# A new table of order, engines and buffers for a two-layer interleaved attention kernel on one core

## The chip, the cores and the metric

The kernel runs on one core of one Trainium2 chip. A core has five engines with queues of their own: PE (TensorE, matrix products into PSUM), DVE (VectorE), ACT (ScalarE), POOL (GpSimd) and SP (SyncE, which here issues nearly all DMAs). The profile shows PE's weight loads as PEld. Each engine works through its queue in order, and waits at an instruction until the semaphores named there have reached a value. The metric is the time of one execution on the device, in microseconds (us); less is better. The median of three runs of the kernel before is 483.39 us.

## The reference

The input x has 2048 tokens of 512 values (bf16), and there are 32 heads of 16 values. Four blocks follow each other, A B A B, each as `x = x + block(layernorm(x))`; both A blocks share their weights, and so do both B blocks.

```
A: q, k, v = x@wq, x@wk, x@wv; four segments of 512 tokens, in order:
     p     = softmax(q k^T * scale + causal mask)      within the segment
     a_mem = phi(q) M / (phi(q) z + 1e-6)              phi(t) = t + 1 if t > 0 else exp(t)
     o     = sigmoid(beta) * a_mem + (1 - sigmoid(beta)) * (p v)
     M, z  = M + phi(k)^T v, z + sum phi(k)            for the next segment
   result o @ wo
B: q, k, v = x@wqkv; pq, pk = q w_phi, k w_phi         per head
     phi_q = [softmax(pq), softmax(-pq)], phi_k likewise
     kv    = sum over ALL tokens of phi_k^T v; z = sum of phi_k
     o     = phi_q kv / (phi_q z + 1e-6)
   result o @ wo
```

The sum over all tokens in B means that no query of B can be finished before the keys of all 2048 tokens are done. This cuts the program in three: up to the first such point, from there to the second, and the end.

## The kernel before, in words

Tokens lie in 16 tiles of 128, four tiles to a segment. The activations X stay in SBUF for the whole run. The program is first recorded as a list of 2864 operations with their reads and writes (`Graph.op`), and each operation knows on which engines it can run. An operation is one instruction on DVE, ACT or POOL, a small group of matmuls on PE, or a DMA. Then `Graph.place` reads a packed table, `ORDER`, with three things for the whole program:

```
order = [self.ops[i] for i in np.frombuffer(raw, "<u2", n)]     # the order of all operations
o.seq, o.eng = k, ENGS[raw[2 * n + o.id]]                        # the engine of each
slots = dict(zip(tiles, raw[3 * n:]))                            # the buffer of each tile
```

`Graph.emit` (line 190) cuts this one order into five queues and sets a wait wherever an operation needs a result of another queue, or a buffer which the tile before it in the same buffer (its `base`) still uses. So the table alone settles what stands behind what on each engine, and which wait ends when.

The steps that matter here, with their places:

- Layer norm, `ln` (line 574): DVE takes statistics of a tile of X (line 577) and combines them (line 578), POOL (or ACT for the first four tiles) takes the root, DVE normalises (lines 594 and 598). The result is transposed by a DMA of SP (`tr`, line 364) or, for some tiles, by PE with an evacuation from PSUM (`tpe`, lines 378, 359 and 360).
- Block A, `a_proj` (line 658): keys and queries of four groups of heads are one pair of operations each (`pair`, lines 330 to 347, eight matmuls in each half, shown at line 341). `evac` (line 358) copies them out of PSUM on ACT (line 359) or DVE (line 360). For each group DVE multiplies the keys by four masks (line 679), which the score products need. V uses the weight WA_v, which POOL or DVE multiplies by a gate first (line 530).
- Block A, `a_att` (line 768): scores on PE (`mm`, line 326), exponentials on ACT (line 351) from PSUM, products with V on PE, the division on DVE (line 847), transposes, output projection and residual (`out_proj`, line 877; the residual is an addition on DVE at line 898 or, where PE has added X itself, a copy).
- Block B: `b_keys` (line 922) and `b_query` (line 987), with exponentials on ACT, sums and products on DVE, and an output projection at the end. The results leave by a DMA of SP for one or two tiles (line 368).

PSUM is four tiles, D0 to D3, of 1024 float32 in each partition, and almost every product goes through one of them. At the start PE multiplies ones for a while (`warm`, line 639: 26 wide operations and some narrower ones) before the first transposes.

The loads of the start are DMAs of SP and ACT at line 457: four single tiles of X, then X in pieces of four tiles (512 KB), then weights, in the table's order.

Of the kernel before, what the change touches and what calls it, by code (L numbers as in the profile page):

```python
# [16 lines left out]
D = 512  # L17
H = 32
# [279 lines left out]
class Kernel:  # L298
# [834 lines left out]
>$jbUTia2NrT*bFujX0lN*opoj1SWniA&0<SfR4M{RVLn^RIzty&#=61^)(r|lVOYslvEHmF3}egLY&L<-W5ZcAn#20AFOZPNvAOIzd&#0OAKS&&u+=OQ+spQ_P!^W
;0tUGtH)MnC0FVQ6!Yej{4TaYX!GTn4BuhkJ0dN8P$`tru7<7lVY#n>U*0Ub)jeTUvAP?k+d{6-LLP3}a$zc+#fwfQ^N<uLx0sWyb3;+%v7=c0!?;r(~f`zO!B&YZA
mQ7~wSw9#LDPc5hfC(@LQo%+T0%Kt+OoMSSp2cRVAq9PB8`wMci6QoeJ}?;8!6LRE5>pad%m_73VI04~2bjnN8vG6xKf)%M0+V4LPGth7vCU8x2Ej%)AIm{S*u(-LH
aWPN4TR}nU<Q0<)uB8jWpQW=+sPzUg6L2KDnM<RgE62E%*Cou4QfIys0;OA9#nz(&;aT~We8vqSs>fZ%78>4W@DcqCM1G*kQib?LudqzVH+%iee4k14$EN)B!T_xFp
CedVLM9-OJNr5fFPI+J7Ez7!yH%)bD;?=fTpkl_CNyo0Y6v>M27GX1;Rm8hycwXEktFXAsk~E5dt9;62eS4#?rtSwgDHyMqCM7;0RlVTVXZsg<04ZBEeDC9Kt{g2nz
# [91 lines left out]
```

## Time and profile before

| what | value |
|---|---|
| runs | 482.28, 483.39 and 484.38 us; median 483.39 |
| profiled execution, first to last instruction | span 481.9 us; no time of its own is listed beside it |
| PE busy | 452.9 us, 94% |
| DVE busy | 438.3 us, 91% |
| ACT busy | 425.9 us, 88% |
| POOL busy | 63.8 us, 13% |
| weight loads of PE (PEld) | 298.4 us, 62% |
| first projection on PE | 13.31 us |
| first score product on PE | 21.16 us |

How to read the profile: busy time counts an engine's own work, not its waits. The end of a matmul is modelled, and matmuls overlap, so PE's busy share says little of how near to its peak PE is; two starts that follow each other say more. A row "x<-y" gives the tile written and the tile read, then count, busy time, mean length in ns, and the idle time just before with what ended it. PEclk is the share of full clock that PE was granted. The chain follows the last instruction back, at each step to what released it.

### The profile page before, as it was taken

Reading aid. Unit: us, or ns where it says so; the run is one execution under the profiler, and the core shown is the slowest. Engines: PE = TensorE matmul, PEld = TensorE weight load, DVE = VectorE, ACT = ScalarE, POOL = GpSimd, SP = SyncE. Lnnn points to the kernel's source line nnn. Section 1 sums busy time; section 2 is a strip of 40 time slices with the busy share of each in tenths; the row PEclk is TensorE's granted clock in tenths of the full one; section 3 lists DMA queues with packets and bytes.
Section 4 is the critical chain, followed back from the end, with each engine's and each line's share of the span. In section 5 each row is a group of like instructions: output and inputs, shape, how many; then the busy total and the mean of one; then the engine's idle time right before and its main releaser. Section 6 shows DMA issues by size and latency. Waiting matters only on the chain.

```text
span 481.9 us, 25218 instructions
## 1 busy us (share of the span) xinstructions
PE 452.9 (94%) x11582; PEld 298.4 (62%) x11582; DVE 438.3 (91%) x920; ACT 425.9 (88%) x560; POOL 63.8 (13%) x145
## 2 busy tenths in 40 slices
PE   8798889999989999998999999999999999999895
PEld 3346665757767677666555677576667666666553
DVE  4998999899889999898999999999999897998883
ACT  2598999999989998578999999999999999776892
POOL 2801120101010110200231041020002020110000
PEclk9999999999999999998999999999999999999799
DMA  8735254350144212200225344432204403100256
GB/s 216 199 83 139 39 90 69 47 86 21 41 68 69 37 15 48 41 1 5 46 52 96 57 72 59 79 67 47 31 4 62 77 16 59 37 12 3 46 93 196
DMA packets 89451, 30.37 MB, mean 63 GB/s; under 512 B 76000, under 2 KB 89344, under 8 KB 89344
## 3 DMA queue, kind: packets, MB, share of 16 engines
q1 hardware_dynamic: 88992, 28.46, 32.1%
q8 instruction: 91, 1.49, 1.3%
q10 hardware_dynamic: 288, 0.26, 0.2%
q0 software_dynamic: 64, 0.02, 0.1%
q14 instruction: 16, 0.13, 0.1%
HBM read 6.32 MB, written 2.10 MB: 17 GB/s over the span
## 4 chain that ended last, share of the span: by engine, by line
PE 54%; DVE 20%; ACT 17%; DMA 3%; issue 2%; SPq 2%; POOL 1%; DVEq 0%
PE D L341 35%; PE D L326 18%; ACT p L351 9%; ACT pF L351 5%; DVE p L635 3%; DVE pQ L679 2%; DVE stats L577 2%; ACT pE L351 2%; SPq L364 2%; DVE p L360 1%; DMA X<-in_A_x_dram 1%; DVE p L598 1%; DVE pK L360 1%; DVE p L847 1%; DMA pX<-p 1%
## 5 line engine op out<-in xcount | busy, mean ns | idle before, releaser
L351 ACT ACTIVATE p<-D 128x1024 bf16<-128x1024 f32 (+1 forms) x276 | 251.5, 956 | 27.5 <-PE D L341 15.9
L351 ACT ACTIVATE pF<-D 128x896 bf16<-128x896 f32 x128 | 117.3, 938 | 2.7 <-PE D L326 2.0
L326 PE MATMUL D<-pK,pQ 64*128 64x256 bf16 (+3 forms) x1536 | 113.9, 243 | 6.1 <-DVE pQ L679 2.3
L326 PEld LDWEIGHTS D<-pK,pQ 64*128 64x128 bf16 x1536 | 54.9, 94 | 45.6 <-ACT p L351 5.8
L326 PE MATMUL D<-pV,pF 64*128 64x34 bf16 x1024 | 75.8, 176 | 1.7 <-ACT pE L351 0.5
L326 PE MATMUL D<-pW,pF 64*128 64x34 bf16 x1024 | 73.0, 176 | 0.5 <-issue 0.5
L585 POOL TENSOR_SCALAR rstd<-mv 128x1 f32<-128x1 f32 x60 | 18.6, 321 | 357.4 <-DVE mv L578 357.4
L341 PE MATMUL D<-pX,WA_k 64*128 64x512 bf16 x256 | 64.7, 376 | 0.7 <-DVE pX L360 0.7
L341 PE MATMUL D<-pX,WA_q 64*128 64x512 bf16 x256 | 64.7, 377 | 0.1
L326 PEld LDWEIGHTS D<-pV,pF 64*128 64x128 bf16 x1024 | 56.8, 93 | 5.3 <-issue 2.2
L326 PEld LDWEIGHTS D<-pW,pF 64*128 64x128 bf16 x1024 | 52.4, 93 | 1.3 <-issue 0.5
L351 ACT ACTIVATE pE<-D 128x768 bf16<-128x768 f32 x64 | 52.5, 830 | 0.8 <-PE D L326 0.4
L326 PE MATMUL D<-pV,p 64*128 64x34 bf16 x1024 | 52.2, 175 | 0.9 <-issue 0.6
L326 PE MATMUL D<-pW,p 64*128 64x34 bf16 x1024 | 51.1, 176 | 0.0
L326 PEld LDWEIGHTS D<-pV,p 64*128 64x128 bf16 x1024 | 46.7, 93 | 2.7 <-ACT p L351 0.5
L326 PE MATMUL D<-tri,two 64*128 64x128 bf16 (+1 forms) x384 | 46.2, 234 | 0.0
L326 PEld LDWEIGHTS D<-pW,p 64*128 64x128 bf16 x1024 | 45.1, 93 | 1.6
L577 DVE BATCH_NORM_STATS2 stats<-X 128x6 f32<-128x512 bf16 x64 | 42.7, 680 | 3.7 <-DMA X<-in_A_x_dram 3.4
L326 PE MATMUL D<-pV,pE 64*128 64x34 bf16 x512 | 45.0, 175 | 0.0
L679 DVE TENSOR_SCALAR pQ<-p,m 128x512 bf16<-128x512 bf16 x128 | 44.2, 366 | 0.1
L326 PE MATMUL D<-pW,pE 64*128 64x34 bf16 x512 | 42.7, 175 | 0.3 <-issue 0.3
L945 DVE TENSOR_REDUCE pS<-p 128x64 f32<-128x1024 bf16 (+1 forms) x36 | 38.6, 1084 | 1.3 <-ACT p L351 1.3
(118 smaller groups left out, 1001.5 us busy)
## 6 DMA issues: line engine op xcount, KB each, us to landing
pW<-pV SPq DMA_DIRECT2D x16, 136.0 KB, 2.8
out_dram<-X SPq DMA_DIRECT2D x7, 256.0 KB, 3.3
X<-in_A_x_dram SPq DMA_DIRECT2D x3, 512.0 KB, 6.4
pX<-in_B_wqkv_dram SPq DMA_DIRECT2D x3, 512.0 KB, 5.2
p<-p SPq DMA_TRANSPOSE x76, 2.6
pX<-p SPq DMA_TRANSPOSE x54, 3.3
WA_k<-in_A_wk_dram SPq DMA_DIRECT2D x2, 256.0 KB, 6.4
WA_q<-in_A_wq_dram SPq DMA_DIRECT2D x2, 256.0 KB, 8.0
```

The lines of the kernel that those rows point to most:

```text
L326: ins = e.matmul(out_ap, lhsT, rhs, start=st, stop=sp, tile_position=(basep(lhsT), basep(out_ap)))
L341: ins = e.matmul(out_ap, lhsT[64 * hf:64 * hf + 64], rhs[64 * hf:64 * hf + 64], start=k == 0 and i == 0, stop=k == 1 and i == len(lists[hf ...
L351: return self.g.op({"act": (dur, lambda e: e.activation(out_ap(), in_ap(), func, scale=scale))}, reads, writes, opens, label=label)
L360: "dve": ((340 if fast else n / 0.96 + 65), lambda e: e.tensor_copy(out_ap(), in_ap()))}
L364: return self.g.op({"sp": (1200.0, lambda e: [e.dma_start(out_ap(), in_ap(), transpose=True)])}, reads, writes, opens, kind="d", lat=1450. ...
L577: v(lambda e: e.bn_stats(self.stats[:, t, :], self.X[:, t, :]), 602, [R("X", t)], [R("st", t)], label="bn")
L585: v(lambda e: e.tensor_scalar(rs, self.mv[:, t, 1:2], LN_EPS, None, op0=ALU.add), 170, [R("mv", t)], [R("rstd", t)], eng="pool", label="rstd")
L598: v(lambda e: e.tensor_scalar(xn.t[:], self.X[:, t, :], self.mv[:, t, 0:1], self.rstd[:, t:t + 1], op0=ALU.subtract, op1=ALU.mult), 300, [ ...
L635: v(lambda e: e.scalar_tensor_tensor(dst.t[:], e_.t[:], 1.0, dst.t[:], op0=ALU.min, op1=ALU.add), 335, [dst, e_], [dst], label="phadd", po ...
L679: fn = lambda e, KM=KM, KT=KT, sl=sl: e.tensor_scalar(KM.t[:, :, sl % 2, :, 64 * (sl // 2):64 * (sl // 2) + 64], KT.t[:].rearrange("p (j h ...
L847: v(lambda e, pvv=pvv, rden=rden, part=part: e.tensor_tensor(part(o).rearrange("p (a h d) -> p a h d", a=2, h=16), pvv()[:, :, :, 0:16], r ...
L945: fn = lambda e, sgn=sgn, eo=eo, Z=Z, n=n: e.tensor_reduce(Z.t[:, 0:64 * n].rearrange("p (k s h) -> p k s h", k=n, s=2)[:, :, sgn, :], eo( ...
```

## The change

The string `ORDER` is replaced; not one line of the program beside it differs. The operations are the same 2864, with the same reads and writes. Decoded, the tables differ so:

- Order: an operation of PE stands 3.3 places from where it stood on its queue on average (at most 29), of ACT 6.1, of DVE 8.5, of SP 5.1, of POOL 4.2.
- Engines: 30 operations change their engine. Copies out of PSUM of 512 columns: 12 from DVE to ACT and 8 from ACT to DVE, transposes with them included; two copies of V (1024 columns) from DVE to ACT; three residual copies of the last 20 us from ACT to DVE; a copy and a fold of weights from DVE to ACT; one gate and two fills with a constant from POOL to DVE.
- Buffers: tiles get other buffers of their pool; the pools and their sizes stay.
- Start: SP issues its two single tiles of X, then four tiles of X, then keys' and queries' weights, WA_v, and the other weights later. DVE takes the statistics of all four single tiles before those of the tiles 4 to 7. The first group's two halves of the key and query projection follow each other on PE, where the second group's first half stood between them. Four of the 26 wide warm-up matmuls stand behind the first transposes.

The diff, cut to its ends (a line is 136 characters of a packed string):

```
--- before.py
+++ after.py
@@ -1127,67 +1127,67 @@
 ORDER = """
-c-rlH1GFW}vTa60y4Ggfwr$(CZQHhO+qP}nw(ag$wYu*)=lb4<KmHrz)!wTzvnn%k=8PGUReP@_tTL;@;<M;1F{{d|vFfY_tI2Ay+N=(%%j&WEtO0At8nMQ#32Vxlv
...
+c-rlH1C%XGw(VN6!dbNo$F^<Twr$(CZQHhO+qP|=^E3B3ef!?q-M_nk|2M{aW4x@Y+>wzHOLMLj5qne;s0>x0DpZ5&Py=d0EvOB3pf1#d`p^IxLL+DlO&~GEhXlYN5fl
...
 """
```

More of the change, by code (lines that the diff above doesn't have):

```diff
@@ L1134 @@
[L1134 to L1137, printed above, removed]
@@ new lines @@
+XFb$-JrBD>dK`_jM`LF~Y!%!TC%b+WE!xfMVGXt{akQ-ORDtHNiUoZ#0!<?8B=7M5haRGEjM23tx*abD~iM{X@C>#N=Au9x6Hp~DcVJ)nK>^K?Tz(-gOYak!y$CCIJ*2
+5n71_iJn&Vv%z7yDr{9F1epzywH+b6_@X!n{}<!$L89kDD<NeK;N`V1LYmyI?2yz_1UH0yU1scaRbXU@6>yd!aOz!Ev||C*m5Mgx?_*a$Jj3(XynF3MRr}bXa$s0zGgD
+N?eEQF%*Je3iifNFbz{<S|sd)lkppV$MH}W%i%&;1jIP2h?Ouo{ea!D7-B<ptbx%nHqFC9I3M4`TbReT!ax*k4ih+^N%k4$vKUw!r{fHq3e%ttmd6TM7wch7tcJBP5mv
+>R7ze9hAZ&yrm>A>X60DCOFe+_=%}^P`Lj!Dxjc^+-#Y1oyw&NmPjInSP+Xp{zKSZO1G=mvTL91C12Cyx#0~_N^whV(Y1S4Zq+yFaqIi{pgoP%?57B<1SI2(_^QD}<Iu
@@ new lines @@
+sH&Yg5hxihQYSj4j1AIT*ub4J-8RwunlY@TZsqYAk4%>v<kmKd~AWya5bjEwQLJ+#oDY6E6P6NCrpaf*=LMS5wHe}K?!g-)?~F<d)$Q`up@TDeHa#JvDs`thJ#|PIIF}
+evns41Ys8|m*cc95VpG<PRb{QPHMYS+>@bVQs<8wtI*Y~PuxTuiC1lswbvB*FAs;)y4zeH?k%ePnSqs*jMZ`#~0lR?Ppe}37Vz7(Ygk8b|co6Hej;s@F#kNB|mWU;0E!
+iP#&DyY3bOjUB0=AGH#wBbiI|&If5{6-g*dn%=Sv-PA@faS*W$Xw$$_lencpA@OUly0GWXD($R)VcyC$JyOgeS2#JI?yBcq}t!!K_%4oyFy>C+o#xvvYVJ(_wn-%m%V9
+Y!J(U?O6xbpM__aaRA%GBEnX-jfJw9tOtwC+Olq}JL}2@v$zzG;?oeeiS1(B*=BYJZ?GM3lO>^~G?d-Ndw7qvV>{S=mYJodm^6&-WV=}ii^5K@EbJ;iz~Ss9%gU~>`?!
@@ new lines @@
+aVV8JXG%g6Sz>zJR#qBHC&JIik1DR!ETWDoH%Uc)==E=xc+aW$=>6Oe>mVwc%%yoE_wGWMA5r1LBd?V@w+2|mKqY%ir}8Q4?2#WG?xwvTeMN9;E1L>Jiw)|ryC>})qZ$
+3656AF>B5C0kA_=m~p`PgzFxjIE?M_!e`p+-xnaqIFb&)ue1tkaeJrREt_sYwAK>sWv5}v^0uEU@fR6J*8)qjxw=^l!~>dMwErJQhMr1nWzV~qh{2cp0f$;1+J%;n1Z#
+XR~QxcvF?<Sy3uIXhI&zN+Dsd04BJ8z*(A1~4$x#)htjb4EE{d4O;nfa(NQ`^+bBCdrX6&V_Olo42_2?Ol$NDqFWC`#PI=fX_K|I;#x#X(rKxNHy`WPxkPgxzx&SBXB7
+9<b*;Tqmuh~*sMuTWDJ*3ZUEE~thv*YxJJ)#qIn$FM&8cF47483Jds2@dvrZkrNQ+cXDRjC}iOyyYxmVv6#II2!pXgKwuVbqt#(-&5QM$u^c&MMJMdPP6jS5}b?p|doR
@@ new lines @@
+hSCI@M1|=b0lj1I*<_kRQ;E@ex<EzfEoG)s^p0{+Q7TPk=r-M<>vV&Na#AkJPo>y#Xv0ghGVDFwqgMPI`#^0u(p}0+1t<>{Bu<5>HNQ!>Xd1QS?fG<iO>gKvePF418ZP
+Jo<)(a;mDi_Fl#S1z`Sg*>vO#<>@5lS|&-8^PEugZLnP=xYxT2Z#l^ReMK8qI8B3ev+cwcVGP+Fdj&nAa7&7pH}9+L255I{+JMn0E(RGc#Ll2nX3@Q(Z&eW#Q>75_n}A
+SWNdgD4lTNWhUVq0^9?59E1xC!T?)=Xv=Eo{v|idDNL#p^-e0cjL)<GM<8W=fn7L?&Cqc3lF8Pd=(GjVW=nX!4(grU>d`h@e&k5n)l+XIpbsb5WbxE=0kZ=UW|t$;+zX
+Ec|jhQ3i15B1#ihG@yUENAH@sv@HCE(=M#8Y9)TiK5nhg;f%5z;l;9P3ac;Qf4lm8i@RGa~k3{QuWSYm<^8$Q6ugI(LP(F=M=TWFKuf(hJIXoPn%d7DXygHx3H}dd2n1
@@ new lines @@
+|&7JPeP(XYq+V5}(Oe@ESZKpUorlEqo<k$QSUMd<l=jqw;7xI$z4S@+o{Ouf=QgI=m5|EY|R~JSJbvBSS2{i8tm=_-0<0*W>m1BEF4J5!?9=K2^lvvH4EEiwB7Ye45zJ
+8}hh3ScHhCycv(f_wXY;9^cFN@%{WLKgJz#oS)za_(2{j;`0Rj5KqXP^K<+pPsC60)BHS7%+K(%`~ttoFY(L#Di08W;tGGuuW_F^%y04Q{3gG_Z}U5Ry12*h^LP9`|Hx
+;Eqw+3)#J}>H;vs*`pYRX-GylfF^9TGH|G|&RSt6A@E>Fm({5k)`U-1|Gi@VKw$zSu-GL3x0r9hEZDxn1vB!oyO(@QJDi?G57F2aa#B7=+|W{Zd-lE^6Mi8&&km@DRs1
+tPMDBBF|DVxd?hvdG0^iHIpO%lIM^L>DncERj`alG$Veu~eiM2}NuXM`V|2L?V$x=9IZ)Zn;dv6=}tCu~lpn+r<u%Oe7a6#6h`B>=t{(UJ(Hji?w2%ST7FAl;W^VC(?^
@@ new lines @@
+lVuQ#dlZd1uvp6DGh}>eO$RJjUin5Z-Bl3!TB8%83GK$qAtH>lui)^B>I4MudQ}T>FD~rgYa;GRGiimUayeulp$m}A&xFE}l{i1*<D=*3%BEKvki-|SjfXFEhisIsuEG
+SBdYqF5YE6a)UB9|yBDu{~Wx+o<oiR*H(xFIfxi{iG-Ckx6uvY0F`D~rqWwR|J1h|036s4nV>T4JNvBp%Bra<jN8YKj`-iX0+_ibArQD6ER8En=9cE$WCW@{l+zPKsNi
+ge)fqsln>1EHCSeA!?{9EE|Z1qLH{Hs>-{vi5M<Q$_nzfXeElPQu2lzAx4U#s+qVWT8qY_skkdjs8gbtIwDHT%i@Zdq$aDQ;+SY7x{1?bnwqYziff{+=p;soYI2IIE{C
+bkVyfyc%Btb2rfe^ci+l2nI4jDj9-^nHAuFm{@|-v!I*LK!yr`u5iJS74Y%b!;0cxOXA>zrBD!weG%Bu>hvMQshsCHtWDy`<L5vs4Ksyc{jYNV>JMya=Aw3?xw%6H<v>
@@ new lines @@
+@8-h8fuKHsh-KV@`sqEdWo?rmh3NPtJNyDd@nwWHR_81*+&cz4`dhdRm73c<vY1hjZ-^SJNZ!VQv1~cbwEv2%hd|?NTOm2<#_c?d=hKbI(1LXQFB#oSx45D&E<XZK-5u
+nReL!>wUF=S2l-MgQXgeY@kxFVPelt=SG*D})pxO24HWg%617y-S1;s4(L^;>FD0p3s<wJ1M~g9Hx7wqaY@`~i)~cBrD>}%JqJeCs_Ns=mp=z$4iLN44juUOvbCFOsQ2
+SI{)lNMY?bUj<L50&=85Kr`l^s+x`B{e7Vf1G8T7=bKWJl>P2y%;hBF2jeB9fdaHmV@SWpw#MRM(qSBiUH4RP|(J*-<?bHMCW$RAt>s30Xz^q?JK(hw7}lsBOwoTUB`3
+M26^4y<H`eN^6~1CXtSADig>^I*N>}534}kOSP1(WU%ZcLu5D^Q3q(BKB78Hqpgl1Bgp!)zHXp<s|fm_3etyEu#TdSs@l4>Jf=>nsJg1IqqXd#YHA~E>1FDaDy@&J6RM
@@ new lines @@
+1kD68paa-(!)8(CNv(Ou*l5mUC6n`CiaLPwRS)fv@Q2FO5JP<N9;71EpKBq3E-RZ^GINhQ;yyUPJ`i<GjD94H6LWU{Z~x|`~*dZ_+7x!fxIN+sLt0Xl`;COhb}Dp>WBM
+fDI_Oy}1Ds(@~-+vvfvpBgF~>0xrXEUU}u(ej)cFDJ<Ix}_c?$I71Syy`7`>;CG3YNfBMe)5K@q%W#Vs)FvLW9hFlwyvn-=(zf>8YwTUE2^%pr$@<e@}9cy7E!4i>YlQ
+{Orn$Oak7bStV7g8)l?_aiS;6xOy5+=bu;~4{*YJI1Jzge(<9_!xmKpoOXO0SQpeCS^-g(9CDiL=YQ0O|Rx9Ohxm|YE@%0YbO+QlcbSgbukI-#3s6drK57t9;s0yQ=sv
+a`XJXY;=8l6@@Q%}@DolZ}bN{!OX<$C!-O_DxyO%2i=btgSi-%&5sb2U^C)9LjJ`AYTBo%L(gT({6;^c&S(PnKQuTjiJl6IMmj(e(y7MIP5D^i(-dE|5L-S?yEj^l05n
@@ new lines @@
+kJY)=d^t`Z)+uEkHC<lRv*ZzdNyjiT&3K(bhnP^4QRh|R)IzyW@7G85F&)ROlKIpGok{1^#vIVr#5F-C*yL9Q)IohkU)G28d3{n}&}Z~%JyV|2@l1S^OD~h*RS|PdU)A
+r_b$vq@HHB0-6W&Bnt7SA5QAIP+O)M2%eNc%^ViQ}%QL#)^HBrx&2~2D=NhdT(OhT1NMKJMHM3dCakcCV#Gg;5lh0Qb>MddU3%|{i+d{T2{I`dx5)`?YE6UF4#=}jIzS
+LW4G%~L%`&(&YlXEjA9H}~~3{Xj=HFZC;(!DLWrOh%K|WY$@9Bo)cr)Km2|{anA$8P#olN2f3;O;VLz<y1M;8ktGG*6(xy^F~KjZ}nZBPZu=FRD6|HXVdp|HZ@PjP+3e
+?lU=7#X;pHSPUX-K^%Gsnls1p`BmG`~&|g&om01-t-_&<i!pzsx^$h((6*nc#akEE)PGwG*944n(pi!SS=gdN#MSavMRT-1ZWHM#VB3<4r)-&}Iy;LvL%k>(a*<>@>O=
@@ new lines @@
+`7PuhZqsUU}Nw();9onb#bUxlJB(#%$0RO$AfYTr#QD3Vq(hRjJJ=bHRMlqfJaz$*k0?^ks9!tk$1(R&~;xGB?c^{Z*6U=9U>@Mw)`^y18N2>)R%Ux?`@IVWzUFVuqW$
+=ANl)?wbeZo33VZsk)|~sc*jP2IiWXWG0&_=7$C|-b^)P%{a4BZ_*RYL^H-bHc!k9vsuqHPt7wk-ApqN%_H;D%rdjhBD2`MGQxOe%-8@MXt(I+CW%^Q8k$CCwLzndHZK
+e_D@=8hUez!)&1>_<Y}MQJcD=x?Gz-l@GsvtlYt1sV+zdAJ%zX3Jd^5F7ZBxe#F&oTKv)=gZQWIo1nssK0*<|LJxn{H3p{;f77PHlSG&}V!y<3O1pG-KrNAK04HjHg--
+kT5Rs5xf9qHSWDnr0@F-Da5GZg!acW~Y(%fZ1hsn}g<%A**b#ZEhmk5c}4=Gv7@M)6%pzhs_TY!G1Qa%n>uqb}-@X7bEN*v)Al%x6_er6g$awG@Z?48`Va$txa?r!?rO
@@ L1191 @@
+QW7{ai%6FBdcm_SZkZoS<M2HtXf7mx*2=q-%*nf4ca^qQ(H9KRLX57~~ZQce-%>&@NfslFZ#2Bm%(2FCY*?IP*#Fb~rBA$?-fyZ9)2!%O{RLzyOb5Hh{SqDwS)Hu*%H`
+mpeW$h1}|)y%K{WgavW*)(SV&fzl<ub;IxGo!<q3{{zG&-bM
 """
```

76 lines of the change are left out of this document (19 added, 57 removed).

## The prediction

> **What bounds the kernel now.** I read the busy shares first, then the chain, then stretches cut at changes of work. From the page (busy us and share of the span, then the chain's shares):
>
> ```profile
> span 481.9 us, 25218 instructions
> PE 452.9 (94%) x11582; PEld 298.4 (62%) x11582; DVE 438.3 (91%) x920; ACT 425.9 (88%) x560; POOL 63.8 (13%) x145
> PE 54%; DVE 20%; ACT 17%; DMA 3%; issue 2%; SPq 2%; POOL 1%; DVEq 0%
> ```
>
> Three engines share the chain; none is slack. The stretches (length, then busy us and instructions of PE, PEld, DVE, ACT and POOL, then PE's granted clock, DMA share, GB/s):
>
> ```profile
> 0.00:12.00 12.00, 10.22 (x94) 4.72 (x94) 5.73 (x18) 3.49 (x11) 2.83 (x14) 1.00 0.83 216
> 12.00:45.00 33.00, 28.01 (x485) 15.60 (x484) 31.30 (x75) 25.37 (x36) 11.03 (x22) 1.00 0.64 154
> 45.00:78.00 33.00, 29.75 (x869) 20.39 (x863) 31.24 (x75) 32.22 (x41) 7.20 (x16) 1.00 0.39 64
> 78.00:130.00 52.00, 50.80 (x1500) 35.15 (x1498) 48.90 (x99) 51.17 (x67) 4.95 (x10) 1.00 0.27 46
> 130.00:190.00 60.00, 57.30 (x1710) 41.47 (x1708) 55.12 (x99) 57.03 (x70) 5.11 (x12) 1.00 0.33 51
> 190.00:220.00 30.00, 29.93 (x596) 19.08 (x593) 27.21 (x51) 20.01 (x24) 3.21 (x8) 1.00 0.10 18
> ```
>
> From 45 to 190 us ACT is busy 140.4 of 145; from 190 to 220 PE is the wall; at the start no engine is full and PE's busy time is warm-up matmuls. So a new order can win at the start, and in the short waits between the three engines, and nowhere much.
>
> **The start.** The load of X is the first thing late, then four mask multiplications (L679) beside POOL's gates (L530). Timeline (start, length, engine, count, idle before), then groups (count, busy us, mean ns):
>
> ```profile
> 3.61 1.28 DVE L577 BATCH_NORM_STATS2 stats<-X 128x6 f32<-128x512 bf16 x2 [0.44 <-DMA X<-in_A_x_dram]
> 7.98 0.69 DVE L577 BATCH_NORM_STATS2 stats<-X 128x6 f32<-128x512 bf16 x1 [3.00 <-DMA X<-in_A_x_dram]
> 8.70 1.89 PE L649 MATMUL D<-onesb 128*128 128x512 bf16 x8
> 11.49 1.10 PE L378 MATMUL D<-ident,p 128*128 128x128 bf16 x12 [0.67 <-DVE p L598]
> 13.31 0.37 PE L341 MATMUL D<-pX,WA_k 64*128 64x512 bf16 x1 [0.72 <-DVE pX L360]
> 16.11 0.60 ACT L359 ACTIVATE p<-D 128x512 bf16<-128x512 f32 x1 [3.27 <-PE D L341]
> 17.08 4.31 DVE L679 TENSOR_SCALAR pQ<-p,m 128x512 bf16<-128x512 bf16 x5
> 21.16 0.39 PE L326 MATMUL D<-pK,pQ 64*128 64x256 bf16 x4 [2.26 <-DVE pQ L679]
> ```
> ```profile
> L530 POOL TENSOR_TENSOR WA_v<-WA_v,gt 128x512 bf16<-128x512 bf16 x4 | 4.3, 1110 | 0.0
> ```
> ```profile
> L679 DVE TENSOR_SCALAR pQ<-p,m 128x512 bf16<-128x512 bf16 x128 | 44.2, 366 | 0.1
> ...
> L634 DVE TENSOR_SCALAR p<-p 128x512 bf16<-128x512 bf16 x24 | 6.7, 281 | 0.0
> ```
>
> Before, SP issues one tile of X, then the 512 KB of tiles 4 to 7, then the last single tile; DVE's third statistics belong to the big load, so DVE stands 3.00 us with single tiles waiting behind. The new table issues the two single tiles first and puts the statistics of all four first on DVE. By the rows (0.69 each, the second pair of tiles a little after the first) the four normalised tiles are ready near 8.5. PE then is the gate: 22 of the 26 wide warm-up matmuls now stand before the transposes. The row at 8.70 gives 8 in 1.89, four of these are moved behind, so the transposes begin at about 9.6; four of them at 0.33 (12 matmuls in 1.10) and a last evacuation of 0.6 give the first projection at 11.75, against 13.31: 1.55 earlier.
>
> The new table also runs both halves of the first K/Q projection before the second projection. Eight matmuls take 0.86:
>
> ```profile
> 29.30 0.87 PE D L341 x8
> ```
>
> so the first evacuation starts at 11.75 + 1.73 = 13.5, not 16.11, and ends near 14.1. Behind it DVE has a short operation (L634) and five of the kind that took 4.31 for five beside the gates. DVE gets there near 14.45: three more statistics of 0.69 and about 1 us of small operations, an estimate from the rows, follow its evacuation of 11.3. One gate goes to DVE and is after these, three stay on POOL (3 x 1.11 us) and begin near 14.8, behind DVE's reciprocal and POOL's own queue (an estimate). At the contended rate the five end at 14.45 + 0.28 + 4.31 = 19.0, less the missing fourth gate 18.5; without contention, at the mean of all 128 (366 ns), 16.6. So the first score matmul comes 2.7 to 4.6 us before 21.16. I take 3.0, near the contended row, because the remaining gates still lie beside them. [...]
>
> ACT is nearly full from this point to 190, so an earlier first exponential moves the stretch as a whole. **Term 1: -3.0** (bounds -1.5 to -4.6).
>
> **Work moved between engines.** Of the operations with a choice, 30 change engine. From 45 to 190 us (times of before) ACT gains four net of 512 columns, from 242 to 418 two of 1024; DVE loses the same. In the last 20 us three residual additions go from ACT to DVE.
>
> ```profile
> L351 ACT ACTIVATE p<-D 128x1024 bf16<-128x1024 f32 x220 | 222.1, 1042 | 24.8 <-PE D L341 14.5 <-PE D L326 8.5
> L359 ACT ACTIVATE p<-D 128x512 bf16<-128x512 f32 x15 | 9.1, 608 | 5.7 <-PE D L341 5.4 <-PE D L867 0.4
> L360 DVE CAST pK<-D 128x512 bf16<-128x512 f32 x27 | 18.3, 680 | 0.2
> L359 ACT ACTIVATE pV<-D 128x1024 bf16<-128x1024 f32 x3 | 3.2, 1062 | 0.0
> L360 DVE CAST pV<-D 128x1024 bf16<-128x1024 f32 x13 | 15.9, 1223 | 2.2 <-PE D L341 2.1
> L898 DVE TENSOR_TENSOR X<-X,D 128x1024 bf16<-128x1024 bf16 x23 | 27.9, 1216 | 4.1 <-PE D L341 3.7
> ```
>
> ACT: 4 x 0.61 + 2 x 1.06 = +4.5 us; DVE: 4 x 0.68 + 2 x 1.22 = -5.2. From 45 to 190 both are 92 to 98% busy, so one's loss is the other's gain; I take the same behind it. **Term 2: 0**, bounds -5.2 and +4.5. The three residuals cost DVE at most 3 x 1.22 where it has room; the end is set by PE's last projections and an ACT residual, which stays on ACT:
>
> ```profile
> 476.45 0.74 PE D L341 x10
> ...
> 477.21 0.60 ACT X L359
> ```
>
> If a DVE residual were late there, the 1.22 is the price. 0.
>
> **Waits between 24 and 441 us.** The new order moves a PE operation 3.3 places on average. Where PE's step was over 0.3 us longer than is usual for its kind, I measured in both orders how much PE work stands between the PE operation that feeds the late producer and the one that waits. 37 such steps hold 20.2 us; the waits as the profile groups them:
>
> ```profile
> PEld D L326 <- ACT p L351: 10.0, 30, 0.9
> PEld D L326 <- ACT pF L351: 6.9, 25, 0.6
> PEld D L326 <- ACT pE L351: 4.1, 14, 0.5
> ...
> PEld D L341 <- DMA pX<-p: 1.6, 1, 1.6
> ```
>
> In 20 pairs the distance grows, which covers 8.6 us of the wait; in 9 it shrinks, by 4.0; in 5, with 2.1 us, the two change places, and I count half. That is -4.6 - 1.0. Against it, PSUM buffers are refilled sooner: the PE work between the last matmul into a buffer and the first of its next use falls short of 1.3 us (an exponential of 1.04, in the fence above, and its hand-over) in 171 uses instead of 167, by 57.2 us in sum instead of 49.0. In before 20.2 us of waits went with 49.0 us of shortness, 0.41 each; 8.2 more cost 3.4. **Term 3: -4.6 - 1.0 + 3.4 = -2.2** (bounds -10.7, all listed waits of the longer and reversed pairs gone at no price, and +8.2, every us of shortness paid and nothing gained).
>
> The one long DMA wait (1.6) came from SP's queue:
>
> ```profile
> 134.06 2.16 SPq L364
> 136.28 4.02 DMA pX<-p
> ```
>
> The transpose of a folded weight stands directly before the tokens that PE waits for. In the new order it stands eight places further forward, but the tokens' normalisation comes after a residual (1.22) on DVE. Half: **term 4: -0.8** (0 to -1.6).
>
> Sum: 481.9 - 3.0 + 0 - 2.2 - 0.8 = 475.9. The median of the runs, 483.39, is 1.5 above the span of the profiled execution, which I keep: **477.4**.
>
> **Rivals.**
> *The waits come back at PSUM* (slower). The four D tiles are the common resource; a wait taken from one hand-over shows up at the next refill. Then the 5.6 and term 4 are nothing, each us of shortness costs a us: -3.0 + 8.2 = +5.2, 488.6. It decides once the price passes 5.4. For it: most long PE waits are on ACT's reads of D. Against: distances from ACT's results to their use are longer in the new order (tenth percentile 2.30 us of PE work, was 2.16).
> *ACT as the bound* (no change). ACT's +4.5 falls where ACT is fullest, DVE's relief is worth nothing: -3.0 + 4.5 = +1.5, 484.9. For it: 140.4 of 145. Against: ACT's waits from 130 to 190 (3 us) can take part of it.
> *The full gain*: contention missed at the start (-4.6), no PSUM price (-5.6), SP's wait gone (-1.6): 470.1 span, 471.6; with DVE relief a little less.
> *The clock.* Two stretches have half clock:
>
> ```profile
> 224.00:228.00 4.00, 3.46 (x40) 2.58 (x42) 3.51 (x8) 3.23 (x7) 0.00 (x0) 0.57 0.00 0
> 446.00:453.00 7.00, 6.29 (x144) 3.59 (x143) 6.52 (x19) 5.54 (x13) 0.00 (x0) 0.51 0.13 26
> ```
>
> Both are where the second layer part waits for all keys, and the order there is almost the same, so I keep them. If they went, the loss of 4 x 0.43 + 7 x 0.49 = 5.1 us goes at most: 472.3. [...]
>
> **Chances.** Forecast 0.42; clock 0.10; full gain 0.10; no change 0.15; slower by PSUM or another queue 0.23. Faster 0.62, same 0.15, slower 0.23, with 0.5% (2.4 us) as about what a measurement tells from no change. The forecast's own range is 472 to 481. For 8 in 10 I go to 467 (below it term 3 must be near its lower bound and another case hold too, under 1 in 10) and to 488, close to the PSUM rival's end, with about 1 in 10 above.
>
> **What would show it.** Statistics without the 3.00 us wait; first projection at about 11.7, first score matmul at 18 to 18.6; ACT near 428 us busy, DVE near 436; the three sums of PEld's waits on ACT together below 21.0; no wait on pX from DMA of over 1 us. I am wrong if those three sums rise, or if ACT's busy share falls while PE's waits on DVE grow: then the tighter refills or DVE's order set the time.

## The result, and the profile after

| | runs | median us | lowest to highest | against before |
|---|---|---|---|---|
| before | 20 | 484.00 | 482.28 to 487.51 | |
| after | 20 | 486.85 | 483.20 to 491.96 | 1.0062 (1.0037 to 1.0087) |
| after, once more | 10 | 487.05 | 485.26 to 490.16 | 1.0087 (1.0052 to 1.0123) |

The last column is a ratio of the runs with its 95% interval; it leaves out the few runs in the slow state, so it is not the quotient of the two medians. The new table is slower by 0.6%, little but clear of the noise, against a forecast of 477.4 and "faster" as the likeliest sign. The granted clock does not separate the two kernels: its median is 0.984 over the 20 runs of after and over the 83 runs of before whose clock is on record. The profiled execution of after took 483.78 us, one of its quickest; a second trace of the same kernel (487 us) is used below for that reason. The page of after, first execution:

```profile
span 482.1 us, 25228 instructions
...
PE 455.8 (95%) x11582; PEld 298.7 (62%) x11582; DVE 439.0 (91%) x918; ACT 428.8 (89%) x565; POOL 59.4 (12%) x142
...
PE 63%; ACT 24%; DVE 7%; DMA 3%; issue 2%; DVEq 0%
```

Its stretches, columns as in the prediction:

```profile
0.00:12.00 12.00, 10.56 (x97) 4.98 (x98) 5.92 (x21) 4.42 (x13) 3.06 (x15) 1.00 0.81 220
12.00:45.00 33.00, 30.29 (x592) 17.02 (x590) 32.18 (x81) 28.28 (x39) 11.27 (x22) 1.00 0.59 137
45.00:78.00 33.00, 31.52 (x826) 20.49 (x824) 30.49 (x69) 32.50 (x44) 5.66 (x10) 1.00 0.46 65
...
190.00:220.00 30.00, 28.69 (x576) 18.10 (x570) 26.86 (x52) 21.67 (x29) 3.05 (x8) 1.00 0.12 20
```

From 12 to 45 us PE gets 592 matmuls done instead of 485: the start gained what was meant. Its timeline (start, length, engine, count, idle before):

```profile
3.83 1.88 DVE L577 BATCH_NORM_STATS2 stats<-X 128x6 f32<-128x512 bf16 x3 [2.26 <-DMA X<-in_A_x_dram]
...
9.99 0.83 PE L378 MATMUL D<-ident,p 128*128 128x128 bf16 x12
...
12.36 0.37 PE L341 MATMUL D<-pX,WA_k 64*128 64x512 bf16 x1
...
16.30 0.87 DVE L679 TENSOR_SCALAR pQ<-p,m 128x512 bf16<-128x512 bf16 x3
...
17.07 3.58 POOL L530 TENSOR_TENSOR WA_v<-WA_v,gt 128x512 bf16<-128x512 bf16 x3
...
17.22 0.36 PE L326 MATMUL D<-pK,pQ 64*128 64x256 bf16 x4
```

The first score product starts 3.9 us earlier (17.22 against 21.16). The mask multiplications of the first group end (17.17) as POOL's gates begin (17.07), so three of them take 0.87, where five took 4.31 in before. What DVE does beside the gates now pays instead: one L634 took 1.14, against a mean of 0.28 in the prediction's row.

```profile
18.60 1.14 DVE L634 TENSOR_SCALAR p<-p 128x512 bf16<-128x512 bf16 x1
```

Then PE's waits from 222 to 442 us (us in total, times, longest), in the second trace of after and in before:

```profile
PEld D L326 <- issue: 4.7, 10, 0.9
PEld D L341 <- issue: 4.5, 10, 1.8
...
PEld D L326 <- ACT p L351: 3.5, 12, 0.7
PEld D L326 <- ACT pF L351: 3.2, 12, 0.7
...
PE D L326 <- issue: 2.9, 5, 0.8
...
PE D L341 <- DMA pX<-p: 1.7, 1, 1.7
```
```profile
PEld D L326 <- ACT p L351: 4.0, 14, 0.4
PEld D L326 <- ACT pF L351: 3.6, 12, 0.6
PEld D L326 <- ACT pE L351: 2.2, 6, 0.5
PEld D L341 <- issue: 2.1, 8, 0.4
PEld D L326 <- issue: 1.9, 4, 0.7
...
PE D L326 <- issue: 1.1, 2, 0.6
```

In before, hand-overs from ACT lead these rows. In after "issue" leads them: PE waits for nothing that the profile names, for 2.9 us instead of 1.1, and its weight loads for 9.2 instead of 4.0 (a wait of both stands in both rows). Of the 9.2, 1.75 is the wait that PE's own row puts down to a DMA: the weight loads' row names no releaser for it. In the first trace the weight loads' two rows are 7.5 in sum. What this is, the experiments had to tell.

### The profile page after: what moved, and what is told of

The parts are those of the page before. It is cut to its first block, busy times and chain, and to the rows that moved or that the text cites. A ratio compares the mean times of both kernels' runs of the same rounds, so it can differ in the third digit from the quotient of the medians.

```text
span 482.1 us, 25228 instructions
## 1 busy us (share of the span) xinstructions
PE 455.8 (95%) x11582; PEld 298.7 (62%) x11582; DVE 439.0 (91%) x918; ACT 428.8 (89%) x565; POOL 59.4 (12%) x142
## 3 DMA queue, kind: packets, MB, share of 16 engines
q8 instruction: 91, 1.49, 1.3%
## 4 chain that ended last, share of the span: by engine, by line
PE 63%; ACT 24%; DVE 7%; DMA 3%; issue 2%; DVEq 0%
PE D L341 40%; PE D L326 19%; ACT p L351 10%; ACT pF L351 8%; ACT pE L351 4%; DMA p<-p 2%; PE D L649 2%; PE D L867 1%; DVE p L635 1%; DMA pX<-p 1%; ACT pS L351 1%; PE D L378 1%; DVE stats L577 1%; DVE pQ L679 1%; DVE p L1043 1%
## 5 line engine op out<-in xcount | busy, mean ns | idle before, releaser
L585 POOL TENSOR_SCALAR rstd<-mv 128x1 f32<-128x1 f32 x60 | 15.6, 263 | 362.7 <-DVE mv L578 352.8
L326 PE MATMUL D<-pV,p 64*128 64x34 bf16 x1024 | 53.4, 176 | 1.4 <-issue 1.4
L326 PE MATMUL D<-pW,p 64*128 64x34 bf16 x1024 | 52.3, 176 | 0.0
L326 PEld LDWEIGHTS D<-pV,p 64*128 64x128 bf16 x1024 | 47.5, 93 | 4.9 <-issue 1.7
L326 PEld LDWEIGHTS D<-pW,p 64*128 64x128 bf16 x1024 | 46.1, 93 | 2.3
L679 DVE TENSOR_SCALAR pQ<-p,m 128x512 bf16<-128x512 bf16 x128 | 40.8, 341 | 0.3
```

The source lines that it names most:

```text
L326: ins = e.matmul(out_ap, lhsT, rhs, start=st, stop=sp, tile_position=(basep(lhsT), basep(out_ap)))
L585: v(lambda e: e.tensor_scalar(rs, self.mv[:, t, 1:2], LN_EPS, None, op0=ALU.add), 170, [R("mv", t)], [R("rstd", t)], eng="pool", label="rstd")
L679: fn = lambda e, KM=KM, KT=KT, sl=sl: e.tensor_scalar(KM.t[:, :, sl % 2, :, 64 * (sl // 2):64 * (sl // 2) + 64], KT.t[:].rearrange("p (j h ...
```

## The experiments

### Where the time goes

Four tables made of the two. An operation keeps the place and engine that its table gives it, and tiles share buffers as there (behind a cut the buffers of a pool are numbered anew); the first two are cut at a time, the others take the engines of one and the order and buffers of the other:

```
ORDER of h_a285:    after's entries for what started before 285 us in after's trace, then before's
ORDER of h_b290:    before's entries for what started before 290 us in before's trace, then after's
ORDER of e_engines: before's order and buffers, after's engines (30 operations)
ORDER of e_order:   after's order and buffers, before's engines
```

> Order, engines and buffers of the kernel after for every operation that started before 285 us there, of the kernel before for the rest. Theory 1 (the first 285 us of the change are worth the 3 us that the two traces show there, and the loss comes later): 3 us below before, 481 us. Theory 2 (the operations given to ACT, most of them ahead of 285 us, cost 4.5 us): 0 to 4 us above before. Theory 3 (the new table is more easily disturbed everywhere, so that its typical run is slower than its best): about before or 1 us above it, with a wide spread.

> The other way round: the table of before for all that started before 290 us there, of after for the rest. Theory 1: all of the loss is here: 3 us above before if its best run counts, up to 6 above, 487 to 490 us. Theory 2: only seven of the thirty changed engines are in this part: within 1 us of before. Theory 3: 1 to 3 us above before, spread wide.

> Before's order and buffers, and after's engine for each of the 30 operations that change it. Term 2 of the prediction: 0, within 1.5 us of before. Theory 2: +2 to +4.5 us. Theories 1 and 3 need nothing here: 0.

> After's order and buffers with before's engine for all 30 operations. Theory 2: faster than after by 2 to 4.5 us, so faster than before, 482 to 484 us. Theory 1: about after's time, 487 us, since the loss is one of order. Theory 3: about after's time, spread wide.

| kernel | median us | ratio to before |
|---|---|---|
| h_a285 | 483.49 | 0.9997 (0.9968 to 1.0027) |
| h_b290 | 498.28 | 1.029 (1.0252 to 1.0327) |
| e_engines | 508.94 | 1.0489 (1.0437 to 1.0541) |
| e_order | 498.13 | 1.0299 (1.0262 to 1.0335) |

Theory 3 fits the first; no theory had the other three. Engines and order are worth nothing apart: 30 engines moved in an unmoved order cost 25.6 us, some 0.85 each, and the new order with the old engines costs 14.8. So "the engine moves are the loss" falls: taking them out of after makes it 11 us slower. The cut at 290 us cost 14.9, of which 6.3 came right at the seam by PE's progress; a table cut in the middle of a stretch tests the seam. The two stand-stills, where PE waits for all keys, are better places: both tables have the same operations ahead of them.

```
ORDER of s_abb: after's entries up to the first Zq group, then before's    (216 us)
ORDER of s_baa: before's up to there, then after's
ORDER of s_aab: after's up to the Zq groups of the second layer, then before's  (442 us)
ORDER of s_bba: before's up to there, then after's
```

> The table cut where TensorE stands still between the stages (after the last operation ahead of the first Zq group; both tables have the same operations ahead of that point): after's table for the first of the three stretches, before's for the second and third. Theory P (place: the start is worth the 3 us that the profiled runs show, the loss lies in the second stretch): 481 us, ratio 0.994. Theory F (the new table's first stretch often falls back by 1 to 2.5 us, as the run of the first 285 us showed): 483 us, ratio 0.997 to 1.000. Theory C (each part fits only the rest of its own table): above before by 5 us and more.

> Before's table for the first stretch, after's for the second and third. Theory P: 487 to 490 us, 3 us above before in the best runs and up to 6 in the typical one, since the head's gain is missing from after's 486.9. Theory F: 488 us. Theory C: 495 us and more, as with the cut at 290 us.

> After's table for the first and second stretch, before's for the third (from the second stand-still at 442 us on). The two profiled runs were 0.1 us apart at that point and 0.2 us apart at the end, so theory P: after's own time, 486 to 487 us. If the three residuals that go from ACT to DVE in the third stretch cost what the changed engines cost alone in the run with after's engines (two waits of 3.3 us there): 3 us or more below after, 483 us.

> Before's table for the first and second stretch, after's for the third. Theory P: before's time within 1 us. If the moved residuals are the loss: 3 us or more above before, 487 us.

Measured: s_abb 482.60 (0.9967, 0.9945 to 0.9990), s_baa 490.49 (1.0141, 1.0100 to 1.0182), s_aab 485.71 (1.0032, 1.0007 to 1.0057), s_bba 485.12 (1.0044, 1.0010 to 1.0079). Theory P has the places right and the seams cost little: the first stretch of the new table is better and the second worse. For the size of the first stretch's gain theory F was nearer: 483, where P had 481. The third is no better: the interval of s_bba lies above 1, by 0.8 us of the medians. Two of these were followed up, the kernel after for a full second trace and s_abb because it beats both:

> After itself, unchanged, for a second trace of the whole kernel: by the five traces of its stretches, 213 us for the first stretch, 232 for the second and 34 for the third, with 3.4 to 5 us of waits at borders in the second and a wait of 1 to 2 us for a transpose near 328 us; 486 to 487 us.

> The table with after's first stretch and before's second and third once more, as the candidate that beats both: 482 to 483 us, ratio 0.995 to 0.998.

after_again 487.05 (1.0087, above), as expected. s_abb_again 482.85, 0.9979 (0.9952 to 1.0007): the two measurements of this table together put it 0.2 to 0.3% below before, at the edge of what can be told, and about 1% below after.

Every trace now holds three stretches, and several traces have the same table in one. Their lengths, from PE's first matmul to the last key products (some 2.2 us ahead of the first Zq group), to the second layer's first Zq group, and to PE's last matmul, in us:

| table of the stretch | first | second | third |
|---|---|---|---|
| before's | 213.8 to 215.6, mean 214.7 (5 traces) | 226.8 to 228.2, mean 227.6 (4) | 33.8 (4) |
| after's | 211.8 to 216.4, mean 213.7 (9) | 229.7 to 232.4, mean 231.6 (5) | 33.6 (5) |
| difference | -1.0 | +4.1 | -0.2 |

What follows PE's last matmul, a residual and the last store, takes 3.3 to 4.8 us with before's table (mean 4.2) and 4.8 to 5.0 with after's (4.9). So the sum is -1.0 + 4.1 - 0.2 + 0.7 = 3.6, where the medians differ by 2.9 (486.85 - 484.00); a few traces of each give no closer agreement. The half clock at the start of the second stretch (a granted 0.50, from 224.4 to 227.6 us in before and from 221.8 to 225.1 in after) is not its loss: it lasts 3.4 or 6.8 us in the traces of both tables, 5.1 on average with before's and 4.8 with after's. After's first trace has the 229.7, the one quick second stretch of five; that is why its page shows no loss.

Of each step of PE that took longer than is usual for its kind I worked out, from the starts in the traces and the program's reads, writes and buffers, what it had waited for. Means over the same traces:

| PE's longer steps, us | first, before to after | second, before to after |
|---|---|---|
| refill of a PSUM tile that ACT reads | 4.4 to 6.5 | 6.9 to 8.4 |
| refill of one that DVE reads | 4.2 to 3.0 | 2.1 to 1.6 |
| data from ACT or DVE | 4.6 to 2.0 | 2.4 to 1.7 |
| data from a DMA of SP | 0.7 to 1.4 | 1.1 to 1.8 |
| no releaser ("issue") | 7.0 to 6.2 | 3.6 to 6.7 |
| steps late by less than 0.12 | 3.7 to 4.3 | 3.6 to 3.5 |
| sum | 24.6 to 23.4 | 19.7 to 23.8 |

Three quarters of the second stretch's loss, 3.1 of 4.1, has no releaser.

### What the waits without a releaser are

One of them in the second trace of after, in the timeline of PE and in that of its weight loads:

```profile
405.43 0.19 PE L326 MATMUL D<-pW,pF 64*128 64x34 bf16 x2 [0.74 <-issue]
```
```profile
405.43 0.10 PEld L326 LDWEIGHTS D<-pW,pF 64*128 64x128 bf16 x2 [0.84 <-issue]
```

The queue that loads instructions (packets, MB, share), between 401.30 and 404.30 us and in the whole run:

```profile
q8 instruction: 1, 0.02, 2.9%
```
```profile
q8 instruction: 91, 1.49, 1.3%
```

PE stops in the middle of a group whose data are long there: in after's first trace, where the same stop ends at 401.36, ACT had written the last pF by 399.95. The run loads instructions 91 times, 1.49 MB, so 16.4 KB each; PE has 2 x 11582 matmul and weight-load instructions and 117 to 137 others, some 23,300 in all: 64 bytes each, and a load for each 256. The load ahead of this stop landed at 403.94, 1.49 us before PE went on. Counting PE's instructions in the order of 16 traces: of 899 gaps over 0.45 us between two weight loads, 292 end 1.1 to 1.75 us behind the landing of such a load, and 141 of these 292 are on positions 192 to 195 of 256, while no other four neighbouring positions hold more than about 15. So PE stands at the border of a block until the next has been loaded. In eight traces (682 loads) the landing comes 2.0 us (median) after PE passed the border before, so PE can pass the next about 3.4 us after that one (an estimate from the two; 2.5 to 4.4 for nine of ten). A block of small matmuls (32 instructions of a Zq group in 0.20 us, at which rate 256 take 1.6) is through sooner. That is theory I. The waits at borders of that kind (a gap over 0.35, less 0.1):

| | first stretch | second stretch |
|---|---|---|
| before's table | 2.8 to 3.9, mean 3.3 | 0.6 to 1.6, mean 1.1 |
| after's table | 1.5 to 3.2, mean 2.2 | 3.5 to 4.4, mean 4.0 |

Three borders carry the second stretch's, near 378, 384 and 401 us: gaps of 0.5 to 1.1 in each of the five traces of after's table, and none in before's. If this is right, a few more instructions in the warm-up, which move all borders and keep the warm-up's length, must change the time a lot:

```
-            unit(128, 512, 1)
+            unit(128, 512 if k < N_WARM - 6 else 64, 1)
...
-                for rows, n, m in (..., (128, 34, 8)):
+                for rows, n, m in (..., (128, 34, 56)):          # a_ph96
-                for rows, n, m in ((64, 51, 12), ...
+                for rows, n, m in ((64, 51, 6), ...              # a_phm24, this alone
```

> After's table unchanged. In the warm-up at the start, 48 more matmuls of 34 columns (96 more instructions on TensorE) and six of the 512-column ones cut to 64 columns, so that the warm-up lasts as long as before. The only thing that changes behind it is where the borders of TensorE's instruction loads (one 16 KB load for 256 instructions) fall in the table. Theory I (TensorE waits at a border when it ran through 256 instructions in less than the 3.4 us or so that the next load takes): worked out from the starts in after's trace with the borders moved by 96 instructions and load times drawn from the traces, the waits at borders go from 8.6 to about 17 us, most of it in the first 216 us: 5 to 9 us slower than after, 492 to 496 us. If instruction loads do not bind (waits without a named releaser are something else): after's time, 487 us within 1.2.

> The counterpart: after's table, and 12 matmuls (24 instructions) fewer in the warm-up. Theory I: 8.4 against 8.6 us of waits at borders by the same working, so after's time, 487 us within 1.2. If it is the changed warm-up itself that costs time in the run with 96 more, this one is changed too.

a_ph96 took 496.80 us, 1.0276 (1.0233 to 1.0318): 10 above after, a little over the forecast. Its "issue" rows from 24 to 226 us, and after's in its first 24 to 216:

```profile
PEld D L326 <- issue: 9.5, 16, 2.7
...
PE D L326 <- issue: 7.2, 7, 2.6
PEld D L341 <- issue: 6.5, 14, 1.2
```
```profile
PEld D L341 <- issue: 2.9, 7, 0.7
PEld D L326 <- issue: 2.8, 7, 0.7
...
PE D L326 <- issue: 1.2, 3, 0.6
```

Borders cost 10.0 us there instead of 2.2, and the first stretch took 223.7, 10.0 more than after's mean. The 2.2 that borders do not explain may be the clock's: this trace has two more stretches of half clock than after's first trace, 6.8 us from 47.5 and 3.4 us from 98.7 (its granted clock is 0.97 from 24 to 216 us, after's 1.00). a_phm24 took 489.97, 1.0126 (1.0091 to 1.0162), 3 above after where 0 was forecast. Its interval touches that of after_again, and its one trace shows 1.4 us of border waits in the first stretch, 5.0 in the second and a span of 484.9. But this is the quickest of its six runs (486.65; the others 489.2 to 495.5), so it does not show where the 3 us are. That this changed warm-up costs something in itself is not excluded.

That shows what the borders can cost, not that they are the difference of the two kernels. For that the borders of the second and third stretch alone were moved, in both tables, by issuing one group four times.

```
     def emit(self):
...
+        zq = next(o for o in order if o.id == 1444)
+        once = zq.ch["pe"][1]
+        zq.ch["pe"] = (zq.ch["pe"][0], lambda e: [once(e) for _ in range(4)][-1])
```

> Before's table unchanged; one Zq group at 220.7 us (32 instructions that write the same values again) is issued four times, so 96 more instructions on TensorE from there on, at the place where TensorE then waits 0.8 us. The first stretch keeps its borders of instruction loads, the second and third have them moved by 96 instructions. Theory I: by the starts in three traces of before's table in that stretch, with load times drawn from the traces, waits at borders go from 3.4 to 8.1 us in the second stretch, and the repeated group and the third stretch cost up to 1.5 more: 488 to 491 us, 5 to 7 above before. If waits at borders are taken up by other waits: within 1.5 us of before.

> The same repeat in after's table. Theory I: the order of after's second stretch suits its borders less to begin with, so moving them costs less: 4.0 to 5.8 us by the same working, and up to 1.5 as in the other: 488.5 to 491 us, 2 to 3.5 above after, and about the time of before with the repeat. If the difference of the two kernels had nothing to do with the borders, this one would stay 3 us above before with the repeat.

| | borders as they are | borders moved by 96 |
|---|---|---|
| before's table: median us | 483.98 | 491.59, 1.0167 (1.0126 to 1.0208) |
| its second stretch; waits at borders there | 227.6; 1.1 | 233.7; 6.3 |
| after's table: median us | 487.05 | 489.37, 1.0114 (1.0072 to 1.0156) |
| its second stretch; waits at borders there | 231.6; 4.0 | 233.4; 4.4 |

Theory I had 5 to 7 and 2 to 3.5: before loses 7.6, after 2.3, and the second stretches are then equally long. The waits from 226 to 442 us, b_ph2 and then a_ph2 (the edit moves line 326 to 329):

```profile
PEld D L329 <- issue: 7.3, 10, 1.5
PE D L329 <- issue: 5.4, 6, 1.4
```
```profile
PEld D L329 <- issue: 4.5, 11, 1.1
...
PE D L329 <- issue: 2.6, 5, 1.0
```

So before's second stretch is short because its dense blocks happen to fit the borders; moved off them, it has no lead, and over the whole run before's table is even the slower one there, with intervals that overlap. This is one other position of the borders, with one trace for each table. Borders account for 5.2 of the 6.1 that before's stretch grew and for 0.4 of after's 1.8; the rest is not taken apart. It holds the repeated group (three times 0.2 us) and the clock: around the repeat, half clock lasts 10.2 us in b_ph2 and 6.8 in a_ph2 (granted clock over the whole trace 0.978 and 0.982).

### Two that told little

```
ORDER of a372: after's entries for what started before 372 us in its trace, then before's
ORDER of a_sp: after's, with SP's  xnT 1792, 1799, 2013, 2019
               issued as           xnT 2013, 1792, 2019, 1799
```

> After's table for what started before 372 us there, before's for the rest. In the three traces that have after's table in the second stretch, the waits at borders of instruction loads near 378, 384 and 401 us sum to 2.5, 2.9 and 2.1 us; the traces with before's table have none there. Theory I: 2 to 2.5 us below after, so 484 to 485 us and about before's time. Theory P with refills as the cause (PSUM waits on ACT spread over the whole stretch, 1.5 us more than before): 1 us below after or less.

> After's table with four DMA transposes in another order on SP: the two that the projection at 328 us reads (issued at 322.5 and 324.1 us in after's trace) go ahead of two that nothing reads before 335 us, one right away and one behind one of these. Theory J (a transpose takes 2.4 us or over 4, and the new table leaves too little room for the long ones): the wait for the transpose at 328 us, 0.4, 1.5 and 1.9 us in three traces of this table, is gone, and the median falls by 0.5 to 1.5 us, to 485.5 to 486.5 us. If this wait only hides another: no change.

a372: 487.07, 1.0064 (1.0027 to 1.0101), no gain. The three border waits are gone from its trace, but the seam made a new one of 1.5 (the weight loads' row) at 377 us, and two transposes were late by 1.76 and 0.92. It settles nothing, which is why the borders were moved instead.

a_sp: 487.42, 1.0090 (1.0052 to 1.0128), no gain either. The wait it aims at, in the second trace of after,

```profile
332.02 1.04 PE L341 MATMUL D<-WB_k,pX 64*128 64x512 bf16 x8 [1.68 <-DMA pX<-p]
```

is gone from its trace; 0.44 with another cause is left. But in this trace another transpose, at 94 us, made PE wait 2.3. Transposes are quick or slow by execution: in each trace 68 to 83 of about 137 take under 3.2 us from issue to landing, mostly 2.4 to 2.6, and 34 to 43 take over 3.8. After's table issues 22 of them less than 4.2 us before their first use, before's 9 (both by the first traces). The means above (+0.7 in each stretch) are what this costs; mending one place of many does not show in the time. What makes a transpose slow is open.

## Why the prediction was wrong

- **Term 1, the start (-3.0): right at the start, and then lost.** The first score product came 3.9 earlier, inside the bounds of the term, but not by the row it was sized with: the mask multiplications ran ahead of the gates (three in 0.87), so the contended rate, 4.31 for five, did not apply to them; the L634 that did run beside the gates took 1.14 instead of 0.28. The first projection came at 12.36, not 11.75. After 60 us of PE's work after's table leads by 3.9 us (means of four and three traces), after 180 us by 1.8. "ACT is nearly full, so an earlier first exponential moves the stretch as a whole" was the failing sentence of this term: refills of PSUM that ACT reads took 2.1 more. On the mean of the traces 1.0 is left.
- **Term 2, engines (0): right only with its order.** ACT is at 428.8 and DVE at 439.0 busy, the forecast 428 and near 436. With its three moved residuals the new table is equal to PE's last matmul and 0.7 us longer behind it; whether the residuals do that is not shown. The price per move in an order that was not made for it is 0.85 us; I had argued from busy shares, which cannot show that.
- **Term 3, waits (-2.2): this is the step that failed; one part was near, one was half its size, one was left out.** Refills of PSUM on ACT's side rose by 2.1 + 1.5 = 3.6 (forecast +3.4, the 0.41 per us of shortness). Data and DVE's refills fell by 1.2 + 2.6 in the first stretch and by 0.5 + 0.7 in the second, 5.0 in all, but about 2.3 of it is the first score product's wait (2.26 in the prediction's row), which is term 1; 2.7 is left of the 5.6 forecast, so longer distances did not cover the waits as reckoned. The part left out stands under "Waits between 24 and 441 us": the views I priced were hand-overs and refills (the 10.0 among them is of the whole run), and the rows "issue" were not priced at all, though on the weight loads alone they come to 9.2 us from 24 to 441 us in before:

```profile
PEld D L326 <- ACT p L351: 7.5, 25, 0.7
...
PEld D L341 <- issue: 4.7, 13, 1.4
PEld D L326 <- issue: 4.5, 11, 0.7
```

  Between the two kernels the waits without a releaser differ by -0.8 in the first stretch and +3.1 in the second, of which the borders of instruction loads are -1.1 and +2.9.
- **Term 4, SP's queue (-0.8): it was chance.** The wait of 1.6 us in before is there in one of five traces of that stretch; its transpose took 4.02 us that time and 2.5 in three of the others. After has its own: DMA waits rose by 1.4, where 0.8 less was forecast.
- **The sum.** By the means of the table of PE's steps, hand-overs and DVE's refills fell by 5.0 where terms 1 and 3 had 8.6; DMA waits came to +1.4 instead of -0.8, waits without a releaser to +2.3 instead of 0, refills on ACT's side to +3.6 instead of +3.4, steps late by little to +0.5. That is +2.8 instead of -6.0. Of the 8.8 between, 3.6 are hand-overs, 2.3 waits without a releaser (1.8 of them borders) and 2.2 transposes. The borders made the second stretch the slower one; without them the new table would by this sum still not be faster, but 1 us slower.
- **The rivals.** The slower one had the place (PSUM) partly right, but it was to decide once the price passed 5.4, and the price was 3.6. "ACT as the bound" named the refills that ate the start, but gave 484.9. The clock kept its two half-clock stretches in after's first trace (a granted 0.50 from 221.8 to 225.1 and from 447.1 to 453.8 us); the second trace (0.984 over its whole span, the first 0.988) has one more, 3.4 us from 22 us on, and so have three of the five traces of before's first stretch, near 20 us. No rival was the instruction load.
- **What would show it.** The sum of PEld's waits on ACT's p, pF and pE fell from 21.0 to 19.2 in after's first trace, as forecast, and no wait on pX of over 1 us is in that trace; a reader of these rows alone would have called the prediction right. The second trace has such a wait (1.68).

With one trace each of two kernels whose runs spread by 5 and 9 us, the lucky trace of after hid the loss as well, though its "issue" rows had risen.

Most of the 91 borders of instruction loads show no wait. But 7 of them in the trace of before cost PE 4.5 us; in the two traces of after 10 and 11 of them cost 5.8 and 6.4 us, and in a_ph96 14 of them cost 14 us. In before's trace and after's first, PE reached 30 borders less than 3.6 us after it had passed the one before, and 14 of these show a wait of over 0.35 us; of the other 150, 4 do.

## What to carry to other kernels

Where PE runs through 256 short instructions in less than the 3.4 us or so of this case, as it does with products of 34 columns here (0.20 us for 32 instructions), look at its "issue" waits and count instructions: if they recur at one position in 256, spreading the dense groups is worth a trial (none was made here), and expect any insertion ahead to move all borders behind it. An order is also tied to where its borders fall and to how long its DMAs take; a piece of it moved into another order can cost more than it brings (the cut at 290 us cost 14.9, the one at 285 us nothing). A transpose may need the room of its longer case, about 4 us here. Compare several traces of a kernel, stretch by stretch, before naming a gain.

## What was not expected of the hardware

- PE's waits at the borders of instruction loads: 2.7 us at one border of a_ph96 near 48 us, with a granted clock of 0.69 from 44 to 55, and 10 us of run time with 96 instructions more in the warm-up.
- DMA transposes of the same kind take 2.4 to 2.6 us or about 4: in each execution 34 to 43 of 137 take over 3.8.
- Thirty operations on another engine, with nothing else changed, cost 25.6 us of 484.
